# Weight conversion popped two pieces a step from step 29 to step 65, and one batch's second mixing half at two tasks a step

## The chip, the cores and the metric

The kernel runs on one core of one Trainium2 chip. The metric is the device time of one launch in microseconds (us), the median of several runs of the same program; lower is better.

## The reference

Three layers follow each other, all in float32. The first is causal attention over 4 batches, 8 heads, 576 positions and head width 64, with a bias from a running sum:

```python
cum = np.cumsum(np.maximum(s, 0.0), axis=-1)
bias = -(cum[:, :, :, None] - cum[:, :, None, :])
scores = np.where(causal, -1e9, scale * q @ k.T + np.minimum(bias, 0.0))   # softmax, then @ v
```

The second takes the attention output as x (4 x 576 x 512) and has two parts, a low-rank mixing over positions and a feed-forward net (FFN) of width 2048:

```python
u = x + ((x.T @ U) @ V).T          # mixing, rank 32
x = u + np.maximum(u @ w_ch1, 0.0) @ w_ch2
```

The third is a mixture of four attention experts of width 64 with top-2 gates over the same 576 positions. The weights U, V, w_ch1 and w_ch2 arrive as 64-bit floats, so the kernel turns them into 32-bit floats itself, by bit operations, and splits each operand of a matmul into a high and a low part (three matmuls stand for one).

## The kernel before

The program is written in an explicit order: each engine works through its instructions in the order in which the Python code records them, and waits where one needs another engine's result. TensorE (PE) does the matmuls and transposes, VectorE (DVE) and ScalarE (ACT) empty its results and do the softmax, GpSimd (POOL) scales the softmax rows and takes the low parts of the FFN weights, and SyncE (SP) issues all DMAs, in one line.

**Steps.** The first phase is a loop (`Attn.run`) over 160 steps, one for each of the 5 row blocks of the 32 heads; two heads make a pair, so a pair is 10 steps and a batch 40. A step records the score matmuls of its block (lines 361 and 362), the mask-and-maximum on DVE (line 372, one per step, so it numbers the steps in a trace), the exponential of the step before (line 379), the transposes (402, 405) and the copies out (85, 87) of the block ten steps back, and one piece of the product with V (line 429). Then it calls `fillers(i)`, which adds other work in three kinds:

- a fixed list by step (`todo`): the loads and the operand copies of the next pair, among them the high parts (line 763, POOL), their three copies to other partitions (`place_high`), the low parts (line 667, DVE) and the four last copies (`rest`, which ends with the bias rows, `HI<-Cd`);
- pieces of the weight conversion: a list `convs` of 148 pieces, of which each step takes one, or two in the dense range;
- tasks of mixing and FFN (`background`), as many as the table `BG` says: 1, 1, 0, 2, 1 for the five steps of a head.

```python
for _ in range(CONVS[FAST[0] < i < FAST[1]][i % NT]):
    if i >= 4 and convs:
        convs.pop(0)()
for _ in range(BG[i % NT]):
    background()
```

**Conversion.** 24 jobs: one for U, three for V, four for each of the FFN weights w0 to w4 (256 columns, 256 KB of 64-bit words each). A job is a load (line 186), two operations on ACT (116, 119), three on DVE (122, 126, 130) and, for w0 to w2, the split into a high part on ACT (197) and a low part on POOL (200); w3 and w4 are split later. The pieces of successive jobs are interleaved so that a job takes six pieces. Four buffers hold loaded words.

**Mixing and FFN.** When the second pair of a batch is done, ten mixing tasks of its first half join the queue `mixq`: three of transposes (236) with a copy and a subtraction (240), one product (248) with two empty tasks around it, and four products with an addition into `uT` (259, 262). When the fourth pair is done, the ten of the second half join, the last four of which also split FFN input (276, 277), and then two entries, the second of which puts 14 FFN tasks on `ffnq`. These are, for each of two chunks of 288 positions: a first product for each of w0, w1, w2 (f0 to f2: 12 matmuls at line 293, a relu on ACT at 297 and its low part on DVE at 298) and a second product for each quarter of the output (d0 to d3: 9 matmuls at 307 and an addition at 822; d0 and d1 also split the next chunk's input). An FFN task is taken only when all four jobs of its weight are converted. `background` takes a mixing task on every second call where an FFN task is ready, and the last four mixing tasks of a second half only when `ffnq` is empty.

After step 171 come the remaining 13 weight slices of the FFN over all positions (lines 1010 and 1028), and the third layer.

Of the kernel before, what the change touches and what calls it, by code (L numbers as in the profile page):

```python
# [23 lines left out]
NT = 5  # L24
# [26 lines left out]

PLAIN = (((0, 0),), ((0, 1),), ((0, 2), (1, -2)), ((1, -1),), ((2, -3),), ((0, 3),), ((0, 4),))
STREAM = (((0, 0), (3, -3)), ((-1, 4),), ((0, 1),), ((0, 2), (1, -2)), ((1, -1),), ((0, 3),))
FAST = (40, 70)
RAWS = 4

ENGA = ('vaaaaa', 'aavaav')
ULA = ("vvvv", "gvgg")
# [13 lines left out]
BG = (1, 1, 0, 2, 1)  # L72
# [22 lines left out]
def f32_stages(nc, pool, width, load, m, n, name, use=None, dest=None, fixed={}, raws=2, wide=1):  # L95

    t_ = {}

    def tile_(tag, dt, bufs=1):
        if tag in fixed:
            fixed[tag].append(fixed[tag].pop(0))
            t_[tag] = fixed[tag][-1][:m, :n].bitcast(dt)
            return t_[tag]
        t_[tag] = pool.tile([P, width], dt, tag=tag, name=f"{tag}_{name}", bufs=bufs)[:m, :n]
        return t_[tag]

    def s0():
        raw = pool.tile([P, width], I64, tag="c_raw", name=f"c_raw_{name}", bufs=raws)[:m, :n]  # L110
        load(raw)
        words = raw.bitcast(U32).rearrange("p (n w) -> p n w", w=2)
        t_["low"], t_["high"] = words[:, :, 0], words[:, :, 1].bitcast(F32)

    def p0():
        nc.scalar.activation(out=tile_("c_g", F32, wide), in_=t_["high"], func=AF.Copy, scale=2.0 ** -112)

    def p1():
        nc.scalar.activation(out=tile_("c_r", U32, wide), in_=t_["low"], func=AF.Copy, scale=2.0 ** -29)

    def v0():
        nc.vector.scalar_tensor_tensor(out=tile_("c_s", U32), in0=t_["c_g"].bitcast(U32), scalar=0x80000000,
                                       in1=t_["c_r"], op0=OP.bitwise_and, op1=OP.bitwise_or)

    def v1():
        nc.vector.tensor_scalar(out=tile_("c_a", U32, 2), in0=t_["c_g"].bitcast(U32), scalar1=3, scalar2=None,
                                op0=OP.logical_shift_left)

    def v2():
        nc.vector.tensor_tensor(out=t_["c_a"] if use else dest().bitcast(U32), in0=t_["c_a"], in1=t_["c_s"],  # L130
                                op=OP.add)

    def v3():
        if use:
            t_["u"] = use(t_["c_a"].bitcast(F32))
            next(t_["u"])

    def v4():
        if use:
            next(t_["u"], None)  # L140

    return [s0, p0, p1, (v0, v1, v2, v3, v4)]


def f32_stream(jobs, order):

    n = len(jobs)
    for i in range(-3, n + 1):
        for pieces in order:
            l = [jobs[i + d][3][x] if x >= 0 else jobs[i + d][x + 3] for d, x in pieces if 0 <= i + d < n]  # L150
            if l:
                def step(l=l):
                    for f in l:
                        f()
                yield step
# [3 lines left out]
def fused_kernel(ctx, tc, qk, v, s, u, vv, w12, wp, out):  # L159
# [19 lines left out]
    def wjobs(f, width, cpool, wpool, room, fixed={}, raws=2, wide=1):  # L179


        def job(c0):
            x, c = divmod(c0, DM)

            def load(raw):
                nc.sync.dma_start(out=raw, in_=w12[f, :, x, c:c + width])

            if f in Wf:
                return f32_stages(nc, cpool, room, load, P, width, f"w{f}_{c0}",
                                  dest=lambda: Wf[f][:, x, c:c + width], fixed=fixed, raws=raws, wide=wide)  # L190

            def use(t):
                if c0 == 0:
                    Wh[f] = wpool().tile([P, 2, DM], F32R, tag="wh", name=f"wh_{f}")
                    Wl[f] = wpool().tile([P, 2, DM], F32R, tag="wl", name=f"wl_{f}")
                wh, wl = Wh[f][:, x, c:c + width], Wl[f][:, x, c:c + width]
                nc.scalar.activation(out=wh, in_=t, func=AF.Copy)  # L197
                yield
                eng = nc.vector if WLE == "v" else nc.gpsimd
                eng.tensor_tensor(out=wl, in0=t, in1=wh.bitcast(F32), op=OP.subtract)  # L200
                full[f] = full.get(f, 0) + width

            return f32_stages(nc, cpool, room, load, P, width, f"w{f}_{c0}", use, fixed=fixed, raws=raws, wide=wide)

        return [job(c0) for c0 in range(0, 2 * DM, width)]
# [120 lines left out]
    class Attn:  # L326
# [122 lines left out]
        def run(self, pair_ready, pv_done, heads, fillers):  # L449
            self.pair_ready, self.pv_done, self.heads = pair_ready, pv_done, heads  # L450
            n = len(self.heads) * NT
            i = 0
            while i < n + self.LAG or self.pvq:
                j = i - self.LAG
                view = self.qk(i // NT, i % NT) if i < n else None
                ps = self.tr(j // NT, j % NT) if 0 <= j < n else None
                if i < n:
                    self.peak(i // NT, i % NT, view)
                if 1 <= i <= n:
                    self.exp((i - 1) // NT, (i - 1) % NT)  # L460
                if ps is not None:
                    self.evac(j // NT, j % NT, ps)
                if i % NT == 1 and 1 < i <= n + 1:
                    self.norm(i // NT - 1)
                if self.pvq:
                    self.pvq.pop(0)()
                split = j // (2 * NT) < self.split
                if 0 <= j < n and j % (2 * NT) == 2 * NT - 3 and split:
                    self.push_pv(j // NT, 0)
                if 0 <= j < n and j % (2 * NT) == 2 * NT - 1:  # L470
                    self.push_pv(j // NT, 1 if split else None)
                fillers(i)
                i += 1
# [210 lines left out]
    with ExitStack() as cx:  # L684
# [14 lines left out]
        def load_v(p):  # L699
            b, pr = divmod(p, NP)  # L700
            Vs[p] = d2.tile([P, NT, P], F32, tag="V", name=f"V_{p}")
            nc.sync.dma_start(out=Vs[p], in_=v[b, pr])
# [142 lines left out]
        def use_v(t, x):  # L845
            cs = slice(THIRD * x, THIRD * x + THIRD)
            nc.scalar.activation(out=V4[:, 0, cs], in_=t, func=AF.Copy)
            yield
            nc.vector.tensor_tensor(out=V4[:, 1, cs], in0=t, in1=V4[:, 0, cs].bitcast(F32), op=OP.subtract)

        def job(load, n, name, use):
            return f32_stages(nc, cv, PIECE, load, P, n, name, use, fixed=fixed, raws=RAWS, wide=2)

        jobs = [job(lambda raw: nc.sync.dma_start(out=raw, in_=u), NT * R, "u", use_u)]
        for x in range(S // THIRD):
            jobs.append(job(lambda raw, x=x: nc.sync.dma_start(out=raw, in_=vv[x]), THIRD, f"v{x}",
                            lambda t, x=x: use_v(t, x)))
        jobs += [j for f in range(FA + GROUPS[0]) for j in wjobs(f, PIECE, cv, lambda: w01p, PIECE, fixed, RAWS, 2)]
        convs = list(f32_stream(jobs, STREAM))
# [7 lines left out]
        def background():  # L867


            turn[0] += 1  # L870
            ffn = ffnq and full.get(ffnq[0][0]) == 2 * DM
            if mixq and (turn[0] % 2 or not ffn) and not (mixq[0][1] and ffnq):
                mixq.pop(0)[0]()
            elif ffn:
                ffnq.pop(0)[1]()
# [37 lines left out]
        def fillers(i):  # L913
            p, r = divmod(i, 10)
            now[0] = i % (2 * NT)
            if r == 6 and p < NPR:
                load_v(p)
            if i < 4:
                for _ in range(2):
                    if preps:  # L920
                        preps.pop(0)()
            for x in todo.pop(i, ()):
                x()
            for _ in range(CONVS[FAST[0] < i < FAST[1]][i % NT]):
                if i >= 4 and convs:
                    convs.pop(0)()
            for _ in range(BG[i % NT]):
                background()

        attn.run(pair_ready, pv_done, heads, fillers)  # L930
# [466 lines left out]
```

## Time and profile before

| | us |
|---|---|
| runs (three) | 840.68, 842.06, 843.66 |
| median | 842.06 |
| profiled execution | 842.4 |
| its span, first to last instruction | 840.6 |
| PE busy, share of the span | 799.4, 95% |
| DVE busy | 526.0, 63% |
| ACT busy | 473.8, 56% |
| POOL busy | 322.0, 38% |
| granted TensorE clock | 1.0 |

The score matmuls of the 160 steps start between 9.5 and 269.6 us of the span. Busy shares are averages over stages that differ: in the first phase DVE and ACT are busy for far more than their average. PE busy is the time covered by matmuls that are pipelined and whose ends are modelled; PEld is the loading of their weights, which runs beside them.

### The profile page before, as it was taken

The numbers are of one execution on the slowest core, as the hardware profiler recorded it, in microseconds if no ns is written. First come the engines' busy times: TensorE is split into PE (matmuls) and PEld (weight loads), VectorE is DVE, ScalarE is ACT, GpSimd is POOL, SyncE is SP. The second block draws the span as 40 slices with busy tenths as digits, with TensorE's granted clock in tenths as the row PEclk, the third lists the DMA queues.
The fourth block names the chain that finished last, engine by engine and source line by source line (L and its number), as shares of the span: only waits on it lengthen the run. The fifth ranks groups of instructions, "written<-read, shape, count | busy, mean of one in ns | idle before, by whom it ended". The sixth has DMA issues, their size and how long they took to land.

```text
span 840.6 us, 17207 instructions
## 1 busy us (share of the span) xinstructions
PE 799.4 (95%) x6028; PEld 740.3 (88%) x6028; DVE 526.0 (63%) x1559; ACT 473.8 (56%) x1406; POOL 322.0 (38%) x483
## 2 busy tenths in 40 slices
PE   3889999999999899999999999999999989999997
PEld 2767779889888799999999999999999989898875
DVE  7779987776775357646554764455456775756541
ACT  5779996666776444434444442443334566655662
POOL 5647664453452334223322432232343043322231
PEclk9999999999999999999999999999999999999999
DMA  7887785745741342112111221210000111111221
GB/s 212 216 228 191 212 219 159 202 127 144 190 117 44 106 146 61 51 27 51 51 51 34 69 64 38 52 39 26 1 1 9 36 33 40 48 52 39 76 66 62
DMA packets 37048, 75.44 MB, mean 90 GB/s; under 512 B 4712, under 2 KB 8296, under 8 KB 36932
## 3 DMA queue, kind: packets, MB, share of 16 engines
q1 hardware_dynamic: 36964, 74.36, 32.5%
q8 instruction: 48, 0.79, 0.4%
q14 instruction: 36, 0.29, 0.1%
HBM read 38.93 MB, written 8.55 MB: 56 GB/s over the span
## 4 chain that ended last, share of the span: by engine, by line
PE 79%; DVE 10%; ACT 5%; DMA 3%; issue 2%; SPq 0%; POOL 0%; ACTq 0%; POOLq 0%; DVEq 0%
PE hps L1010 21%; PE facc L1028 21%; PE pv L429 4%; PE qkp L1237 4%; PE facc L307 3%; PE pv L589 3%; PE ops L1264 3%; PE hps L293 3%; PE t L402 3%; PE t L560 2%; PE vps L1171 2%; PE qk L361 2%; PE qk L362 2%; PE t L405 1%; DVE P L372 1%
## 5 line engine op out<-in xcount | busy, mean ns | idle before, releaser
L277 POOL TENSOR_TENSOR ul<-uT,uh 128x288 fp32r<-128x288 f32 x117 | 94.5, 828 | 163.9 <-ACT uh L276 138.1
L1015 DVE SCALAR_TENSOR_TENSOR hl<-hps,hh 128x288 fp32r<-128x288 f32 x110 | 50.3, 457 | 150.1 <-ACT hh L1014 150.1
L390 POOL TENSOR_SCALAR P<-P,stat 64x64 f32<-64x64 f32 (+4 forms) x160 | 101.7, 651 | 104.3 <-DVE stat L385 44.6
L1014 ACT ACTIVATE hh<-hps 128x288 fp32r<-128x288 f32 x110 | 45.0, 409 | 147.9 <-PE hps L1010 147.7
L85 ACT ACTIVATE pt<-t 64x64 f32<-64x64 f32 (+5 forms) x272 | 89.5, 358 | 42.0 <-PE t L405 29.6
L1010 PE MATMUL hps<-uh,wl 128*128 128x288 f32 x376 | 111.2, 296 | 0.0
L1010 PE MATMUL hps<-ul,wh 128*128 128x288 f32 x376 | 111.1, 296 | 0.0
L1028 PE MATMUL facc<-hh,wh 128*128 128x288 f32 x376 | 111.1, 296 | 0.0
L1010 PE MATMUL hps<-uh,wh 128*128 128x288 f32 x376 | 111.0, 295 | 0.0
L1028 PE MATMUL facc<-hh,wl 128*128 128x288 f32 x376 | 110.9, 295 | 0.0
L1028 PE MATMUL facc<-hl,wh 128*128 128x288 f32 x376 | 110.8, 295 | 0.0
L379 ACT ACTIVATE P<-P,stat 64x64 f32<-64x64 f32 (+4 forms) x160 | 89.2, 558 | 23.2 <-DVE stat L372 21.2
L548 POOL TENSOR_SCALAR P<-P,stat,pt 128x128 f32<-128x128 f32 (+4 forms) x72 | 45.8, 653 | 118.1 <-DVE stat L543 54.1
L372 DVE CUSTOM_DVE_ANT_0 P<-qk,mask 64x64 f32<-64x64 f32 (+4 forms) x160 | 77.4, 484 | 13.7 <-PE t L405 8.7
L361 PE MATMUL qk<-R,L 128*128 128x64 f32 (+2 forms) x192 | 66.3, 349 | 18.3 <-DVE L L750 9.6
L200 POOL TENSOR_TENSOR wl<-c_a_w,wh 128x256 fp32r<-128x256 f32 x56 | 43.8, 784 | 73.2 <-ACT wh L197 70.6
L1010 PEld LDWEIGHTS hps<-uh,wl 128*128 128x128 f32 x376 | 70.9, 189 | 0.0
L1028 PEld LDWEIGHTS facc<-hh,wl 128*128 128x128 f32 x376 | 70.9, 188 | 0.0
L1010 PEld LDWEIGHTS hps<-ul,wh 128*128 128x128 f32 x376 | 70.8, 188 | 0.0
L1028 PEld LDWEIGHTS facc<-hl,wh 128*128 128x128 f32 x376 | 70.8, 188 | 0.0
L1028 PEld LDWEIGHTS facc<-hh,wh 128*128 128x128 f32 x376 | 70.6, 188 | 0.1
L1010 PEld LDWEIGHTS hps<-uh,wh 128*128 128x128 f32 x376 | 70.6, 188 | 0.0
(211 smaller groups left out, 2230.0 us busy)
## 6 DMA issues: line engine op xcount, KB each, us to landing
c_raw_w<-in_w_dram SPq DMA_DIRECT2D x64, 256.0 KB
uT<-in_qk_dram SPq DMA_DIRECT2D x15, 576.0 KB
L<-HI SPq DMA_DIRECT2D x28, 288.0 KB
V<-in_v_dram SPq DMA_DIRECT2D x16, 320.0 KB
R<-HI SPq DMA_DIRECT2D x14, 288.0 KB
R<-uT SPq DMA_DIRECT2D x14, 288.0 KB
L<-uT SPq DMA_DIRECT2D x14, 288.0 KB
aD<-stage SPq DMA_DIRECT2D x6, 576.0 KB
```

The source lines that it names most:

```text
L85: nc.scalar.activation(out=out, in_=in_, func=AF.Copy)
L200: eng.tensor_tensor(out=wl, in0=t, in1=wh.bitcast(F32), op=OP.subtract)
L277: eng.tensor_tensor(out=l_, in0=src, in1=h_.bitcast(F32), op=OP.subtract)
L361: nc.tensor.matmul(ps[:, bk, :w], lhsT=q1[:, rows], rhs=k1[:, c0:c0 + w], start=True, stop=False)
L372: nc.vector.tensor_tensor_reduce(out=po, in0=view, in1=mk, scale=-self.scale, scalar=3.0e38, op0=OP.add, op1=OP.min, accum_out=stat[P - M: ...
L379: nc.scalar.activation(out=po, in_=po, func=AF.Exp, scale=-1.0, bias=stat[P - M:, 0, t:t + 1], accum_out=stat[P - M:, 1, t:t + 1])
L390: nc.gpsimd.tensor_scalar(out=pv, in0=pv, scalar1=stat[r0:, 2, t:t + 1], scalar2=1.0 if gate is None else gate(t)[r0:], op0=OP.mult, op1=O ...
L548: nc.gpsimd.tensor_scalar(out=po, in0=po, scalar1=stat[:, 2, s:s + 1], scalar2=1.0 if gate is None else gate(t), op0=OP.mult, op1=OP.mult)
L1010: nc.tensor.matmul(ps, lhsT=w[:, 0, cs], rhs=x, start=i == 0, stop=i == 11)
L1014: nc.scalar.activation(out=hh, in_=ps, func=AF.Relu)
L1015: nc.vector.scalar_tensor_tensor(out=hl, in0=ps, scalar=0.0, in1=hh.bitcast(F32), op0=OP.max, op1=OP.subtract)
L1028: nc.tensor.matmul(accs[c][d], lhsT=w[:, 1, cs], rhs=x, start=f == fs[0] and i == 0, stop=f == fs[-1] and i == 2)
```

## The change

The dense range of the conversion, whose ends are exclusive, is now steps 29 to 65 (before, 41 to 69). A new pair `RUSH` makes `fillers` call `background` twice in each of the steps 52 to 57, whatever `BG` says; step 52 is the one in which the first batch's fourth pair is finished. The lines behind it move down by one.

```diff
-FAST = (40, 70)
+FAST = (28, 66)
 RAWS = 4
+RUSH = (52, 58)
...
-            for _ in range(BG[i % NT]):
+            for _ in range(2 if RUSH[0] <= i < RUSH[1] else BG[i % NT]):
                 background()
```

All 148 pieces of conversion and all tasks stay; only their places change. The conversion's list is used up at step 111 (before, 119).

On DVE, steps 65 and 66 before, where `hl` is the low part after an FFN first product and `c_r_w`, `c_a_w` are of a conversion job:

```order
L372 ISA P_116,stat_110<-qk_0_1438,mask 64x64
L372 ISA stat_110 64x1
L122 SCALAR_TENSOR_TENSOR pt_105<-pt_106,c_r_w_512_1418 128x256
L298 SCALAR_TENSOR_TENSOR hl_1_1467<-hps_1_1453,hh_1_1466 128x288
L372 ISA P_116,stat_110<-qk_1_1470,mask 128x192
L372 ISA stat_110 128x1
L384 TENSOR_SCALAR stat_108<-stat_108 128x5
L385 RECIPROCAL stat_108<-stat_108 128x5
L126 TENSOR_SCALAR c_a_w_512_1490<-pt_106 128x256
L130 ISA c_a_w_512_1490<-c_a_w_512_1490,pt_105 128x512
```

Steps 65 and 66 on DVE now, where `stage` is the result of an FFN second product and `ul` the low part of the next chunk's input:

```order
L373 ISA P_116,stat_110<-qk_0_1477,mask 64x64
L373 ISA stat_110 64x1
L123 SCALAR_TENSOR_TENSOR pt_105<-pt_106,c_r_w_0_1474 128x256
L299 SCALAR_TENSOR_TENSOR hl_2_1506<-hps_2_1492,hh_2_1505 128x288
L373 ISA P_116,stat_110<-qk_1_1509,mask 128x192
L373 ISA stat_110 128x1
L385 TENSOR_SCALAR stat_108<-stat_108 128x5
L386 RECIPROCAL stat_108<-stat_108 128x5
L127 TENSOR_SCALAR c_a_w_0_1529<-pt_106 128x256
L823 TENSOR_TENSOR stage_1541<-facc_0_1531,uT 128x288
L278 TENSOR_TENSOR ul_1_1548<-uT,uh_1_1547 128x288
```

The third first product (`hl_2`) is at step 65, where the second was, and the first second product follows at once; before, the third came at step 73.

On SP's line of DMAs, the copies of pair 4's operands (`HI` high parts, `uT` low parts, `Cd` bias rows), before:

```order
L186 DMA c_raw_w_768_618<-in_w_dram 128x256
L626 DMA L_0_122<-HI 64x1152
L626 DMA L_0_119<-HI 64x1152
L626 DMA R_0_121<-HI 64x1152
L626 DMA R_0_121<-uT 64x2x576
L626 DMA L_0_119<-uT 64x2x576
L626 DMA L_0_122<-Cd 2x2x576
L626 DMA HI<-Cd 4x2x576
L697 DMA uT<-in_qk_dram 128x2x576
```

The same stretch now, from the same load on:

```order
L187 DMA c_raw_w_768_618<-in_w_dram 128x256
L627 DMA L_0_122<-HI 64x1152
L627 DMA L_0_119<-HI 64x1152
L627 DMA R_0_121<-HI 64x1152
L187 DMA c_raw_w_0_690<-in_w_dram 128x256
L627 DMA R_0_121<-uT 64x2x576
L627 DMA L_0_119<-uT 64x2x576
L627 DMA L_0_122<-Cd 2x2x576
L627 DMA HI<-Cd 4x2x576
L698 DMA uT<-in_qk_dram 128x2x576
```

A load of weights now stands between the copies of the high parts and those of the low parts.

## Rows read from the trace of the kernel before

**Rows 1.** The page, part 1: busy us (share of the span) xinstructions.

```profile
PE 799.4 (95%) x6028; PEld 740.3 (88%) x6028; DVE 526.0 (63%) x1559; ACT 473.8 (56%) x1406; POOL 322.0 (38%) x483
```

**Rows 2.** The windows view: a stretch in us, its length, busy us of each engine.

```profile
core 0: us, PE busy (x) PEld busy (x) DVE busy (x) ACT busy (x) POOL busy (x), PEclk, DMA share, GB/s
49.80:65.80 16.00, 15.13 (x118) 11.81 (x118) 13.30 (x43) 12.49 (x42) 10.05 (x15) 1.00 0.66 176
65.80:79.00 13.20, 11.30 (x90) 8.92 (x90) 12.84 (x42) 11.95 (x43) 9.50 (x14) 1.00 0.88 240
79.00:106.70 27.70, 25.89 (x195) 20.68 (x190) 25.36 (x78) 25.46 (x84) 18.07 (x25) 1.00 0.74 193
106.70:131.30 24.60, 24.11 (x189) 19.65 (x189) 20.35 (x67) 20.28 (x69) 16.15 (x24) 1.00 0.72 191
131.30:171.70 40.40, 39.44 (x325) 35.67 (x321) 32.25 (x106) 30.21 (x98) 18.89 (x29) 1.00 0.71 191
171.70:218.60 46.90, 46.54 (x376) 42.88 (x378) 32.16 (x109) 31.34 (x101) 20.91 (x34) 1.00 0.53 148
181.70:201.50 19.80, 19.54 (x162) 17.99 (x161) 13.38 (x45) 13.33 (x42) 8.22 (x13) 1.00 0.54 152
218.60:239.10 20.50, 19.52 (x159) 15.63 (x160) 16.21 (x54) 16.02 (x53) 9.78 (x15) 1.00 0.65 170
234.40:252.20 17.80, 17.46 (x142) 16.29 (x139) 12.61 (x43) 13.00 (x42) 9.63 (x14) 1.00 0.43 104
320.00:340.00 20.00, 20.00 (x152) 20.00 (x151) 14.75 (x32) 8.47 (x24) 8.38 (x11) 1.00 0.24 64
```

**Rows 3.** The windows view of line 372 alone.

```profile
131.30:171.70 40.40, 11.33 (x47) 1.00 0.71 191
```

**Rows 4.** The waits view, 79.0 to 106.7: us in total, times, longest.

```profile
ACT P L379 <- DVE stat L372: 1.6, 4, 0.8
```

**Rows 5.** The waits view, 131.3 to 218.6.

```profile
ACT pt L85 <- PE t L405: 14.8, 7, 3.8
DVE stage L822 <- PE facc L307: 9.7, 9, 2.3
```

**Rows 6.** The lines view, 50 to 79, conversion: xcount | busy us, mean ns.

```profile
L116 ACT ACTIVATE pt<-c_raw_w 128x256 f32<-128x256 f32 x5 | 2.2, 432 | 0.0
L119 ACT ACTIVATE c_r_w<-c_raw_w 128x256 uint32<-128x256 uint32 x5 | 2.2, 441 | 0.0
L197 ACT ACTIVATE wh<-c_a_w 128x256 fp32r<-128x256 f32 x4 | 1.6, 409 | 0.0
L122 DVE SCALAR_TENSOR_TENSOR pt<-pt,c_r_w 128x256 uint32<-128x256 uint32 x4 | 1.7, 431 | 0.0
L126 DVE TENSOR_SCALAR c_a_w<-pt 128x256 uint32<-128x256 uint32 x5 | 2.5, 491 | 0.0
L130 DVE CUSTOM_DVE_ANT_0 c_a_w<-c_a_w,pt 128x512 uint16<-128x512 uint16 x5 | 3.0, 602 | 0.1
```

**Rows 7.** The lines view, 131.3 to 218.6, FFN.

```profile
L297 ACT ACTIVATE hh<-hps 128x288 fp32r<-128x288 f32 x9 | 3.7, 408 | 2.9 <-PE hps L293 2.8
L298 DVE SCALAR_TENSOR_TENSOR hl<-hps,hh 128x288 fp32r<-128x288 f32 x9 | 4.1, 457 | 7.7 <-ACT hh L297 7.6
L822 DVE TENSOR_TENSOR stage<-facc,uT 128x288 f32<-128x288 f32 x13 | 5.9, 455 | 9.8 <-PE facc L307 9.7
```

**Rows 8.** The timeline of SP and PE near steps 30 and 40.

```profile
44.04 0.78 SPq L626 DMA_DIRECT2D HI<-Cd  x1
...
49.12 0.27 PE L362 MATMUL qk<-HI,L 68*128 68x64 f32 x1 [0.40 <-DMA HI<-Cd]
...
57.91 0.52 SPq L626 DMA_DIRECT2D HI<-Cd  x1
...
64.80 1.19 PE L429 MATMUL pv<-pt,V 128*64 128x288 f32 x8
```

## The prediction

> **What bounds the kernel now.** The page's busy shares come first, because they mislead here: PE is at 95% of the span [rows 1], which looks like a kernel with nothing but PE in it. The windows view by stretch comes second [rows 2]. Its stretches are whole numbers of steps: line 372 runs once a step and its accumulator read once more, so 47 instructions in 131.3 to 171.7 are 23 steps and one that reaches in [rows 3]. The stretches are steps 30-39, 40-49, 50-65, 66-80, 81-103 and 104-129, and then, as models, 110-119, 130-142 and 140-149. The last row is the later FFN, where PE never stops: 152 matmuls of 288 columns in 20 us, 0.1316 us each. So a first product of 12 matmuls costs PE 1.58 us and a second product of 9 costs 1.18.
>
> From these rows the reader should see two regimes. In steps 40-65 DVE and ACT are the bound: 12.84 and 11.95 of 13.2 us, then 25.36 and 25.46 of 27.7 [rows 2], and the waits view agrees, since ACT's largest wait there is 1.6 us, for DVE [rows 4]. In steps 81-129 DVE falls to 80% and 69% while PE's weight loads rise from 75% to 88% and 91% [rows 2], and now DVE and ACT wait for PE: 14.8 us for transposes and 9.7 for second products [rows 5]. Steps 66-80 are the change from one to the other. After step 129 neither kernel has a task waiting until pair 11 is done at step 132, and the order from there on is the same but for two tasks that change places and one that is done earlier. So what the change is worth is the time at which step 130 starts, 218.6 us now; the rest of the span is shifted by it.
>
> **The change part by part.** Popping the two queues step by step through both programs gives the contents of each stretch.
>
> *Steps 30-49 and the pops beside them.* Steps 29-40 take one more piece each, 12 pieces, which is two jobs. A job costs ACT 0.432 + 0.441 + 0.409 = 1.28 us and DVE 0.431 + 0.491 + 0.602 = 1.52 [rows 6]; two jobs cost DVE 3.0. Steps 30-39 get ten of the twelve pieces: DVE goes from 13.30 to 15.8 us of work in 16.0 us. At the 97% that steps 40-49 reach with DVE (12.84 of 13.2) that needs 16.3 us; but part of DVE's idle time there lies behind late operands and stays. I take +0.8, and +0.4 for the two pieces outside. Bounds: 0 (all of it falls into the 2.7 us that DVE idles) and +3.0 (none does). **+1.2.**
>
> *The loads.* A load of 256 KB now stands between pair 4's high copies and its low copies on SP, and the next ones come three to six steps earlier. The copies behind it end with the bias rows, issued at 57.91. At step 30 the same copy was issued at 44.04, and PE waited for it until 49.12, 5.1 us [rows 8]. So pair 4's lands at about 63.0, while PE is busy with products until about 66 and step 40 begins then [rows 8]: some 2.8 us to spare. One load in the line would have to delay it by more than that, and DMA's share in steps 30-39 is 0.66, the lowest of the early rows. I price it at 0, with 1.5 us as the other end.
>
> *Steps 50-65.* The ten mixing tasks of the second half, the two empty entries and f0, f1 were spread over steps 53-65; now all twelve queue entries are in steps 52-57, f0 and f1 at 58, and steps 59-64 have no task, because f2 needs w2, whose last piece is popped at step 65. So the contents of the stretch stay, with f2 added: DVE 0.457, ACT 0.408 [rows 7]. DVE and ACT are at 92% either way, and crowding the work into one half and thinning the other moves no sum; in steps 59-64 PE has idle time that it had in 66-72 before. **+0.5**, from -1 (the last idle 8% shrinks) to +2 (two mixing tasks in a step stall each other).
>
> *Steps 66-80.* Before: f2, d0-d2, three transposes, one product 248. Now: d0-d3, f0-f2, d0-d3 and three transposes. That adds 2 first and 5 second products, 2 x 1.58 + 5 x 1.18 = 9.1 us of PE, and drops the product 248 (10 matmuls, 1.3 at the same rate): +7.8 on PE. DVE gets 2 x 0.457 + 5 x 0.455 = 3.2 [rows 7] and loses four pieces, 1.0: from 20.35 to 22.6 of 24.6. So the stretch becomes one of PE. Models are steps 140-149 (3 first, 3 second products in 17.8 us) and 110-119 (the same and three transposes in 19.8) [rows 2]. One and a half of the first is 26.7 us with 4.5 of each kind; 1.5 first products fewer and 3.5 second more add 1.8: 28.5. From the second, 31.5. Steps 66-80 lie nearer to the first, since both models hold the long product with V done in one piece, and up to pair 6 it comes in two. I take 29.0, **+4.4**; ends +2.2 (only DVE counts) and +6.9.
>
> By PE's own busy time, 24.11 of 24.6, this stretch has no room at all, and the 7.8 us would be added in full. The Trainium skill's page "Perfetto Trace Analysis", section "Identifying the Most-Contended Engine", says that matmul busy time does not show how near PE is to its limit, since matmuls are pipelined, and that the share of LDWEIGHTS does. By that, 19.65 of 24.6, there are 4.95 us of room, and the stretch would grow by 2.9 instead of 4.4; the sum below would then be +0.3, by busy time +5.2. The models from the trace stand between them, nearer to the skill's.
>
> *Steps 81-103.* Before: d3 of the first chunk, f0-f2 and d0-d3 of the second (3 first and 5 second products), and mixing. Now mixing alone (the product 248 too): PE loses 3 x 1.58 + 5 x 1.18 - 1.3 = 9.3 us, and steps 88-92 have no task, because pair 7 is not done. With that little, PE is no longer the bound and the 9.3 us don't come back in full. Models: steps 130-142, mixing alone, 1.58 us a step (20.5 / 13); steps 30-39 with one piece a step and mixing, 1.60; the fastest, steps 40-49, 1.32 [rows 2]. At 1.59, 23 steps take 36.5 us instead of 40.4: **-3.9**. Ends: -7.0 (1.45 a step) and -2.4 (1.65).
>
> *Steps 104-129.* The same 14 FFN and 10 mixing tasks, two steps ahead, and eight pieces of conversion fewer on DVE and ACT, which are not the bound: **-0.4**, from -1.5 to +0.5.
>
> Sum: 1.2 + 0.5 + 4.4 - 3.9 - 0.4 = +1.8 us. The profiled execution took 842.4 us, 1.8 above its span and 0.3 above the median of the runs; against the median the sum gives 843.9, and I say 844.0. About 0.3%, 2.5 us, is what a measurement of this kernel can tell from no change, so the likeliest case is none that can be told, on the slow side. Its own range is 841 to 846.5.
>
> **The rivals.**
>
> *Faster: the light steps run fast.* If steps 81-103 keep the pace of 1.45, because without FFN nothing in PE's line delays the transposes that ACT waited 14.8 us for, they give back 7.0. With steps 66-80 at 28.0 (+3.4) and the early pops in DVE's idle time (+0.3) the sum is 0.3 + 0.5 + 3.4 - 7.0 - 0.7 = -3.5: 838.6. For it: steps 40-49 with two pieces a step do 1.32. Against it: they have two mixing tasks where 81-103 have some eighteen, and steps 130-142, with mixing and no pieces at all, do 1.58.
>
> *Slower: FFN is bunched and then runs dry.* The mechanism is the place of the 7 FFN tasks: they meet in steps 66-80, which become purely a matter of PE at the pace of steps 110-119 (+6.5), and are missing in 88-92 and 128-129, where a step can't get shorter than its softmax (-3.0). With +1.5 in steps 30-49 and +0.8 in 50-65 and -0.4 that is +5.4: 847.4. It decides once steps 66-80 take over 30.5 us. For it: PE's matmuls in the two models are at 98% busy; against it: steps 66-80 have spare DVE time and short products with V.
>
> *Late operands.* The load in front of pair 4's low copies delays them past the 2.8 us; then PE waits at step 40, as it did at step 30, and so again at pair 5: +1.5 each at most, on top of +1.8: 847. Nothing in the row of step 40 speaks for it but the delay of 5.1 us at step 30.
>
> *The second knob does nothing.* Done at two tasks a step or not, f2 waits for w2 until step 65, so the mixing's early end is worth one step at most; then the conversion alone decides, +1.2 against some of the -0.4, and the time is 843. This falls into the likeliest case.
>
> **How the numbers follow.** Likeliest, with the idle second knob inside it: 0.45. Faster: 0.24. Slower by bunching: 0.25; late operands: 0.06. From the likeliest case a few parts in 45 pass the bound of 2.5 us, more upward than downward, since its sum is at +1.8: faster by over 0.3% 0.25, within 0.3% 0.41, slower by over 0.3% 0.34. The sums of all low and all high ends are -7 and +11; such a meeting is rare, and 8 in 10 lie between -5.5 and +7.5: 836.5 to 849.5.
>
> **What would show it right or wrong.** In the changed profile step 40 should start near 67 us, step 66 near 108.4, step 81 near 137.4, step 104 near 174 and step 130 near 220.4. PE should show no wait for `HI<-Cd` at step 40. Weight loads of PE should rise in steps 66-80 to about 90% and fall in 81-103 to about 76%, as in steps 130-142. The forecast is wrong if step 130 starts before 216 or after 223, if steps 30-49 grow by over 3 us, or if the part after step 130 changes its length by more than 1 us.

## The result and the profile after

The changed kernel takes 850.67 us (median of 4 runs, 847.65 to 855.62), the kernel before 842.86 on the same chip (840.68 to 844.29): ratio 1.0096, 95% interval 1.0072 to 1.0119. It is slower, and above the range of 836.5 to 849.5 us. The profiled execution took 852.27 us with a span of 850.2; before, 842.4 and 840.6. The two profiles lie 9.6 us apart and the medians 7.8: the traced execution of the kernel before has no fall of the TensorE clock ahead of its last 0.7 us, while other executions of it have mean granted clocks down to 0.992, so a difference between two profiles is not yet the price in the median.

The page of the changed kernel, parts 1 and 2: busy time (share of the span), and the granted TensorE clock in 40 slices.

```profile
PE 805.5 (95%) x6028; PEld 742.2 (87%) x6028; DVE 524.7 (62%) x1559; ACT 474.6 (56%) x1406; POOL 319.9 (38%) x483
...
PEclk9999999999899999999999999999999999999999
```

Every engine has as many instructions as before. The windows view of the changed kernel (same columns as [rows 2]) has the steps 30-39, 40-49, 50-65, 66-80, 81-103, 104-129 and 130-140; the last two rows are steps 66-72 and 4 us behind the start of step 130. Lines are one higher than before.

```profile
50.60:67.50 16.90, 15.35 (x119) 11.72 (x115) 15.86 (x48) 15.14 (x51) 11.66 (x17) 1.00 0.79 197
67.50:80.50 13.00, 10.87 (x86) 8.64 (x88) 12.67 (x41) 11.62 (x42) 9.35 (x14) 1.00 0.83 215
80.50:109.80 29.30, 27.07 (x207) 22.38 (x203) 25.92 (x81) 25.86 (x85) 18.24 (x25) 1.00 0.73 191
109.80:140.70 30.90, 30.81 (x245) 27.33 (x244) 20.69 (x70) 20.54 (x66) 13.64 (x22) 1.00 0.60 165
140.70:176.30 35.60, 33.77 (x256) 26.84 (x255) 29.92 (x101) 28.53 (x93) 18.34 (x29) 1.00 0.71 187
176.30:225.10 48.80, 46.61 (x372) 42.74 (x371) 30.33 (x103) 31.24 (x102) 19.80 (x33) 0.98 0.55 151
225.10:246.00 20.90, 20.25 (x151) 15.39 (x150) 14.12 (x49) 14.05 (x47) 8.18 (x14) 0.88 0.54 144
...
109.80:126.40 16.60, 16.51 (x131) 14.55 (x131) 10.23 (x36) 9.63 (x32) 9.59 (x15) 1.00 0.67 183
...
224.00:228.00 4.00, 3.91 (x23) 2.95 (x25) 1.78 (x9) 1.47 (x6) 1.13 (x2) 0.50 0.44 166
```

| steps | before | after | difference | forecast |
|---|---|---|---|---|
| up to 29 | 49.8 | 50.6 | +0.8 | +0.4 |
| 30-49 | 29.2 | 29.9 | +0.7 | +0.8 |
| 50-65 | 27.7 | 29.3 | +1.6 | +0.5 |
| 66-80 | 24.6 | 30.9 | +6.3 | +4.4 |
| 81-103 | 40.4 | 35.6 | -4.8 | -3.9 |
| 104-129 | 46.9 | 48.8 | +1.9 | -0.4 |
| 130 to the end | 622.0 | 625.1 | +3.1 | 0 |

Two places stand out: steps 66-80, and the surroundings of step 130, where nothing was expected.

**Steps 66-72** hold all of the +6.3 and 1.0 us more, since the eight behind them give that back. The same seven steps in the kernel before:

```profile
106.70:116.00 9.30, 9.07 (x74) 6.78 (x73) 9.07 (x32) 8.93 (x33) 7.09 (x11) 1.00 0.71 201
```

They go from 9.3 to 16.6 us. DVE was busy for 9.07 of 9.3 us, 98% (PE's matmuls for as much, its weight loads for 73%); now DVE is at 62%, PE at 99% and the weight loads at 88%. The waits view of the changed kernel, 109.8 to 140.7 (what waits, for whom: us in total, times, longest), says the same: DVE and ACT now wait for the FFN.

```profile
DVE hl L299 <- ACT hh L298: 5.2, 4, 2.2
...
ACT hh L298 <- PE hps L294: 4.9, 2, 2.9
DVE stage L823 <- PE facc L308: 3.0, 5, 0.8
```

What was added there is in the lines view of the same stretch (operation, xcount | busy us, mean ns); these are one of three matmuls of each kind of FFN product:

```profile
L294 PE MATMUL hps<-uh,wh 128*128 128x288 f32 x10 | 3.2, 325 | 0.0
L308 PE MATMUL facc<-hh,wh 128*128 128x288 f32 x10 | 3.2, 324 | 0.4 <-ACT hh L298 0.4
```

That is 60 FFN matmuls, where the kernel before had 4 in these steps. At 0.1316 us each, the 56 more are 7.4 us, and the steps are 7.3 longer.

**Step 130.** Timelines (start, length, engine, line, operation). On SP in the changed kernel, pair 13's operands; step 130 is the first that reads them:

```profile
216.68 0.57 SPq L825 DMA_DIRECT2D aD<-stage  x1
217.35 0.61 SPq L627 DMA_DIRECT2D R<-uT  x1
218.02 1.05 SPq L627 DMA_DIRECT2D L<-uT  x1
219.12 1.11 SPq L627 DMA_DIRECT2D L<-Cd  x1
220.34 1.01 SPq L627 DMA_DIRECT2D HI<-Cd  x1
```

On SP in the kernel before:

```profile
208.97 0.62 SPq L626 DMA_DIRECT2D R<-uT  x1
209.63 0.62 SPq L626 DMA_DIRECT2D L<-uT  x1
210.29 0.72 SPq L626 DMA_DIRECT2D L<-Cd  x1
211.11 1.05 SPq L626 DMA_DIRECT2D HI<-Cd  x1
...
216.88 0.57 SPq L824 DMA_DIRECT2D aD<-stage  x1
```

`aD<-stage` stores a finished FFN chunk. It is recorded when the chunk's last second product is emptied: step 128 before, step 123 now, since the FFN is ahead. The copies `R<-uT` to `HI<-Cd` are recorded at step 124. So the store now stands ahead of them, SP waits for it, and the copies wait with it. SP's waits and the low parts on DVE, in the changed kernel:

```profile
SPq L825 <- DVE stage L823: 6.9, 1, 6.9
```

```profile
214.49 0.76 DVE L668 TENSOR_TENSOR uT<-uT,HI 128x576 fp32r<-128x576 f32 x1
```

The low parts are there at 215.25; the first copy leaves at 217.35, 2.1 us later. Step 128 has one mixing task left and step 129 no task at all, so PE has nothing to cover that with. PE in the changed kernel ([..] is idle time and what ended it):

```profile
221.24 0.27 PE L406 MATMUL t<-ident,P 128*64 128x128 f32 x1
223.27 0.42 PE L362 MATMUL qk<-R,L 128*128 128x64 f32 x1 [1.76 <-DMA L<-uT]
224.09 0.39 PE L363 MATMUL qk<-HI,L 68*128 68x64 f32 x1 [0.39 <-issue]
...
226.14 4.84 PE L430 MATMUL pv<-pt,V 128*64 128x288 f32 x32
```

The wait costs 2.1 us. Behind it the granted clock is at 0.50 (1.2 GHz) from 223.1 to 229.95, and the 32 matmuls of a product with V take 4.84 us; before they take 2.99:

```profile
218.52 2.99 PE L429 MATMUL pv<-pt,V 128*64 128x288 f32 x32
```

### The profile page after: what moved, and what is told of

Same layout as the page of the kernel before. It is cut to its first block, busy times and chain, and to the rows that moved or that the text cites. A ratio compares the mean times of both kernels' runs of the same rounds, so it can differ in the third digit from the quotient of the medians.

```text
span 850.2 us, 17207 instructions
## 1 busy us (share of the span) xinstructions
PE 805.5 (95%) x6028; PEld 742.2 (87%) x6028; DVE 524.7 (62%) x1559; ACT 474.6 (56%) x1406; POOL 319.9 (38%) x483
## 4 chain that ended last, share of the span: by engine, by line
PE 80%; DVE 10%; ACT 5%; issue 3%; DMA 2%; SPq 0%; POOL 0%; ACTq 0%; DVEq 0%; POOLq 0%
PE hps L1011 21%; PE facc L1029 20%; PE pv L430 5%; PE qkp L1238 4%; PE hps L294 3%; PE t L403 3%; PE facc L308 3%; PE pv L590 3%; PE ops L1265 3%; PE t L561 2%; PE vps L1172 2%; PE qk L362 2%; PE qk L363 2%; PE t L406 1%; DVE P L373 1%
## 5 line engine op out<-in xcount | busy, mean ns | idle before, releaser
L391 POOL TENSOR_SCALAR P<-P,stat 64x64 f32<-64x64 f32 (+4 forms) x160 | 99.5, 636 | 118.7 <-DVE stat L386 41.5
L373 DVE CUSTOM_DVE_ANT_0 P<-qk,mask 64x64 f32<-64x64 f32 (+4 forms) x160 | 77.3, 484 | 19.9 <-PE t L406 11.8
```

Source lines behind the costliest of these rows:

```text
L373: nc.vector.tensor_tensor_reduce(out=po, in0=view, in1=mk, scale=-self.scale, scalar=3.0e38, op0=OP.add, op1=OP.min, accum_out=stat[P - M: ...
L391: nc.gpsimd.tensor_scalar(out=pv, in0=pv, scalar1=stat[r0:, 2, t:t + 1], scalar2=1.0 if gate is None else gate(t)[r0:], op0=OP.mult, op1=O ...
```

## The experiments

Times are medians, ratios are to the kernel before on the same chip, with 95% intervals. Lengths of steps are from each kernel's profile.

**The two halves of the change.** E1 has the early conversion alone (without `RUSH`), E2 `RUSH` alone (`FAST` as before), E9 the early conversion with the first batch's FFN kept out of steps 66-72.

```diff
 E2: -FAST = (28, 66)                                        +FAST = (40, 70)
 E9: -ffn = ffnq and full.get(ffnq[0][0]) == 2 * DM
     +ffn = ffnq and full.get(ffnq[0][0]) == 2 * DM and not 66 <= stp[0] < 73
```

> The earlier dense range alone, without the doubled mixing. Theory A (bunching): the FFN of the first batch starts at step 66 instead of 73, and nine of its twelve remaining tasks stand in steps 66 to 79, so steps 66 to 80 grow by 3 to 5 us and the light steps 81 to 103 give back about 4. Theory B (the store in front): the store of the second batch's second chunk is still recorded at step 123, ahead of pair 13's low copies at step 124, so PE waits at step 130 for 2 us or more and the clock may fall there, 2.5 to 5.5 us. A and B together: 846 to 850 us. Theory C (conversion is dear where DVE is the bound, and nothing else matters): 844 us, without a wait at step 130.

> The doubled mixing of steps 52 to 57 alone, with the dense range of before. Two FFN tasks come earlier (steps 58 and 59), the third waits for its weight until step 73 as before. Theory A (bunching) and theory B (the store in front, which here is recorded at step 126, behind pair 13's copies) both expect no change: 841 to 844 us, step 130 at 217 to 221 us of the span. If crowding the mixing into steps that DVE and ACT bind costs by itself, steps 50 to 65 grow by 1.5 us as in the changed kernel, and the time is 844 to 845.

> The earlier dense range alone, with every FFN and mixing task in the step where the kernel before has it (the third FFN task is held until step 73). What is left is the price of early conversion. Theory C (twelve pieces more in steps 29 to 40, on DVE and ACT that are the bound there, and no return later, where PE is the bound): steps 30 to 66 grow by 1.5 to 2.5 us, nothing is given back, 844.5 to 846. As I predicted (1.2 us, 0.4 of it given back): 843.5 to 844.5. If conversion has no price: 842 to 843.5.

E1: 853.64 us, 1.0125 (1.0104 to 1.0145): over the 846 to 850 of its two theories together, and no better than the whole change (0.3% above it, with intervals that overlap). E2: 843.99, 1.0003 (0.9992 to 1.0015). E9: 843.98, 1.0009 (0.9998 to 1.0020); its steps 66-72 in the windows view:

```profile
108.20:116.90 8.70, 8.49 (x71) 6.28 (x70) 7.69 (x30) 7.34 (x26) 6.61 (x11) 1.00 0.69 191
```

So `RUSH` alone is worth nothing, and converting early costs some 0.8 us by itself, with an interval that reaches down to no cost. What costs is that finished weights let the FFN tasks come earlier: in E1's trace the third one is emptied at step 66 (before, 73) and the last at step 83 (before, 95). Why E1 is no better than the whole change was open until E13.

**What sets the length of steps 66-72.** E8 leaves out two of the three matmuls of each FFN product of the first batch (the correcting ones). E6 empties each FFN result one step later than it is made, E7 does that in the kernel before.

```diff
 E8: +ws = ((Wh[f], h_), (Wh[f], l_), (Wl[f], h_))[:1 if c < 2 else 3]
 E6, E7: +late.append(empty)        # run at the next step
```

> The changed kernel with a third of the matmuls of the first batch's 14 FFN tasks (the high parts' product alone; the two correcting products are left out), and ACT's, DVE's and POOL's work as it is. In steps 66 to 80 PE does 9.5 us less. If PE's matmuls are what those steps last for: they shrink by 8 to 9.5 us, to 22 us. If the hand-offs between PE, ACT and DVE are: they shrink by under 5 us, and 26 us or more stay.

> The changed kernel, but the operations that empty an FFN task's result (relu and low part, or the addition into stage) are recorded in the next step, behind that step's mask and maximum, not right behind the task's matmuls. Hand-off theory (an FFN task stands in line between two steps on PE, ACT and DVE alike, so that DVE and ACT idle through its matmuls): steps 66 to 80 shrink from 31 to 26 to 28 us, and the total to 843 to 847. If steps 66 to 80 are simply full of PE work: no gain beyond 1 us, 849 to 851.

> The kernel before with the emptying of FFN results one step later, as in the run above. Hand-off theory: the steps with FFN tasks (73 to 95, 106 to 128, 144 to 161) get shorter by 0.1 to 0.3 us each, 835 to 841 us. If PE's own work is the bound there: 842 to 845.

E8's steps 66-72:

```profile
107.90:119.70 11.80, 11.80 (x98) 9.86 (x96) 10.47 (x36) 9.72 (x34) 9.72 (x15) 1.00 0.71 198
```

They take 11.8 us instead of 16.6, 4.8 less, for 5.3 us of PE work taken out (40 of the 60 matmuls at 0.1316); steps 66-80 take 23.5 instead of 30.9. So PE's matmuls set these steps, in the main: the 7.4 us that steps 66-80 give back are a little less than the 8 to 9.5 of that forecast, and more than the 5 of the other. Its time, 846.94 us, 1.0045 (1.0023 to 1.0067), gives back only 4.3 us by the ratios, of the 12.6 taken out of the whole batch (two thirds of 6 x 1.58 + 8 x 1.18); its ten runs lie between 842.12 (the traced one) and 850.39 us, with mean granted clocks of 0.988 to 0.996, so the total is not a clean price. E6: 850.40, 1.0090 (1.0068 to 1.0112), no gain, and steps 66-72 take 19.1 us. Its total holds a second thing: one step later, the last store stands behind pair 13's copies (on SP at 222.10 us, the first of the low copies at 218.24), so steps 125-134 take 13.7 us instead of 18.9, while emptying late makes steps 66-80 3.1 us longer. E7: 846.12, 1.0033 (1.0022 to 1.0044), slower and above both of its forecasts; why is open. The theory that DVE and ACT wait because a result is emptied too soon falls.

**The store in SP's line.** E5 moves one store, that of the second batch's second chunk, behind pair 13's copies; E3 delays all stores to the sixth step of a pair; E11 leaves the store and adds 18 matmuls, whose result nothing reads, at step 129.

```diff
 E5: +if c == 3:
     +    todo.setdefault(125, []).append(store)
     +else:
     +    store()
 E3: +stores.append((c, stage["t"]))      # handed to SP at r == 5
 E11: +if i == 129:
      +    for _ in range(18):
      +        nc.tensor.matmul(ps, lhsT=V4[:, 0, :P], rhs=V4[:, 0, :CH], start=True, stop=True)
```

> The changed kernel with the store of the fourth chunk alone handed to SP at step 125, behind pair 13's last copies; the three other stores stay where the change has them, so no store is forced to stand right before the next chunk's first result, as in the kernel with all stores late. Store in front: from step 125 to step 135 the time is that of the kernel before (15.5 us) instead of 19.0, PE has no wait for L<-uT at step 130, the clock doesn't fall there, and the total is 2 to 5 us under the changed kernel: 845.5 to 848.5. If the wait at step 130 was hidden anyway: 850.

> The changed kernel with one thing moved: the store of an FFN chunk is handed to SP at the sixth step of a pair, behind the last copies of the next pair's operands, instead of at once. Theory B: pair 13's low copies are issued as soon as they are computed, PE does not wait for them at step 130 and the granted clock stays at 1.0 there; 2.5 to 5.5 us less than the changed kernel, 845 to 848 us. Theory A alone (all of the loss is from bunching): no difference, 849 to 851.

> The changed kernel with 18 matmuls added at step 129, whose result nobody reads (2.4 us of PE in front of the scores of step 130). PE works while it would wait for pair 13's low copies. If the fall of the granted clock behind that wait is what costs 3 us after step 130: the clock stays at 1.0 there, step 131 takes 2.7 us instead of 5.6, and the total is 1.5 to 3 us under the changed kernel, 847.5 to 849, though work was added. If the clock falls for another reason, or costs nothing: 850 to 852.

E5: 847.79 us, 1.0051 (1.0032 to 1.0069). SP and PE in its timeline:

```profile
216.71 0.62 SPq L627 DMA_DIRECT2D R<-uT  x1
...
220.57 1.39 SPq L826 DMA_DIRECT2D aD<-stage  x1
```

```profile
222.70 0.28 PE L362 MATMUL qk<-R,L 128*128 128x64 f32 x1
```

No wait at step 130 and no fall of the clock there; steps 125-134 take 13.8 us instead of 18.9 (before, 15.5). That is 5.1 us in the profiles; the ratios differ by 0.45%, 3.8 us. The steps 66-72 stay at 16.7.

E3: 856.44, 1.0159 (1.0144 to 1.0174), above both of its forecasts. The gain at step 130 is there too (steps 125-134 take 13.8), but `stage` has one buffer, and with the store just ahead of the next chunk's first result, that result waits for it: steps 73-74 take 10.1 us instead of 3.8. The run shows the price of another wait and is no verdict on the store. E11: 850.55, 1.0094 (1.0080 to 1.0109). In its profile PE has no wait for a DMA at step 130 and the clock stays at 1.00:

```profile
221.64 2.61 PE L928 MATMUL fill<-V 128*128 128x288 f32 x18
...
225.54 2.99 PE L430 MATMUL pv<-pt,V 128*64 128x288 f32 x32
```

Steps 125-134 take 16.1 us, so with the gap filled the clock stays, as the first forecast has it, but the ratio is that of the changed kernel, as the second has it: the filling takes 2.6 us itself, and two of the changed kernel's four runs have mean granted clocks of 0.998 and 1.000, so the fall is not in each of them.

The runs with a mean granted clock of 1.000 show the store's price almost without falls: 847.65 us for the change, 845.34 for E5, and 841.97 and 841.77 for the kernel before, measured beside E5. By these single runs the store costs 2.3 us, close to PE's wait of 2.1, and the falls behind that wait would make up the rest of the 3.8.

**The conversion alone, with two stores moved.** In E1's trace the same thing happens twice. At step 90, SP and then PE:

```profile
144.76 0.57 SPq L824 DMA_DIRECT2D aD<-stage  x1
145.38 0.63 SPq L626 DMA_DIRECT2D R<-uT  x1
```

```profile
151.32 0.27 PE L361 MATMUL qk<-R,L 128*128 128x64 f32 x1 [1.40 <-DMA L<-uT]
152.47 0.39 PE L362 MATMUL qk<-HI,L 68*128 68x64 f32 x1 [0.88 <-DMA HI<-Cd]
```

Behind it the clock is at 0.50 from 152.2 to 159.0, and again from 227.3 to 234.1 behind step 130. In the changed kernel the store near step 90 stands ahead of the copies too, but leaves before they are ready:

```profile
140.81 1.14 SPq L825 DMA_DIRECT2D aD<-stage  x1
...
145.58 0.62 SPq L627 DMA_DIRECT2D R<-uT  x1
```

E13 is E1 with both stores behind the copies:

```diff
+if c in (1, 3):
+    todo.setdefault({1: 85, 3: 125}[c], []).append(store)
```

> Only the dense conversion from step 29 to step 65, as in the first experiment, and two of the stores of FFN chunks put behind the operand copies of pairs 9 and 13 on SP's line (steps 85 and 125). In the first experiment's profile PE waits 1.4 + 0.9 us at step 90 for copies that stand behind a store, and at step 130 again, and the granted clock falls to 0.5 for 6.8 us behind each; steps 88 to 93 gain 1.9 us on before, where the changed kernel's give back 3.3, and steps 125 to 135 lose 3.5. If the stores in SP's line are why the conversion alone is slower than the whole change, both waits and both falls go, steps 88 to 93 give back about 3, steps 125 to 135 lose nothing, and the time is 845 to 847.5 (+0.3% to +0.55%). If the conversion costs this by itself, the waits go and the time stays above 850.

E13: 848.09 us, 1.0048 (1.0034 to 1.0061). On SP and PE at step 90:

```profile
145.52 0.62 SPq L626 DMA_DIRECT2D R<-uT  x1
...
149.39 0.61 SPq L825 DMA_DIRECT2D aD<-stage  x1
```

```profile
152.22 0.27 PE L361 MATMUL qk<-R,L 128*128 128x64 f32 x1
```

Both waits and both falls are gone. Against before, steps 88-92 give back 3.2 us where E1's lose 1.9; steps 125-134 give back 1.8 where E1's lose 3.5. The median is 0.6 us above the range that the store theory gave, and its ratio inside it; the other theory wanted more than 850. With the stores out of the way the conversion alone (1.0048) and the whole change (E5, 1.0051) are the same within their intervals: that is the price of the earlier FFN and conversion, and E9's 1.0009 is the conversion's part in it.

**Versions that might gain.** E4 is the change with no FFN task in steps 59-72, E10 is E5 with an FFN task in every second of these steps, E12 converts later than before (`FAST = (44, 74)`, no `RUSH`).

```diff
 E4:  +... and not 59 <= stp[0] < 73
 E10: +... and (mixq or stp[0] % 2 or not 59 <= stp[0] < 73)
```

> The changed kernel, but no FFN task is taken in steps 59 to 72, so that the third one comes at step 73 as before. The conversion is early and the mixing doubled as in the change; FFN is spread as before, and the second batch's last store is behind pair 13's copies. Theory A: steps 66 to 80 return to about 25 us and the time to 842 to 845. Theory C (early conversion costs): 1 to 3 us stay, 844 to 846. If neither bunching nor the store is the cause, it stays at 849 to 851.

> The changed kernel with the fourth chunk's store late, and the first batch's FFN taken at every second step in 59 to 72, so that it ends at step 88 instead of 80: less bunched, and no four steps without a task at 88 to 91. If bunching and the empty steps after it (with a falling clock) cost beside the store: 1 to 3 us under the kernel with the one store late, 845 to 846.5. If those cancel and only early conversion is left: the same, 847 to 848.

> The kernel before with the dense range four steps later (steps 45 to 73); FFN and mixing tasks keep their steps. Theory C turned round (pieces of conversion leave the early steps that DVE and ACT bind, and come where PE is the bound or near it): 0.5 to 1.5 us less than before, 841 to 842.5. If the early steps have room for them: no change, 842 to 843.5.

E4: 846.79 us, 1.0045 (1.0023 to 1.0067), between its forecasts. E10: 845.08, 1.0029 (1.0018 to 1.0040), with steps 66-72 at 11.0 and 81-103 at 37.9 us. E12: 842.50, 0.9998 (0.9989 to 1.0007). None beats the kernel before. Spreading the FFN seems to take back part of the loss: E10's ratio is 0.22% under E5's, with intervals that overlap, and in the profiles its steps 66-103 take 1.9 us less than E5's. Why E4 stays at +0.45%, where E2 and E9 with one half of it each are at +0.0 and +0.1, is open: in its profile 2.7 of the 5.0 us that it loses behind the start of step 30 arise in steps 30-39, where the clock falls to 0.50 at 51.6; E9 has the same instructions there and loses 0.8.

## Why the prediction was wrong

By the forecast's own signs it is wrong: step 130 starts at 225.1 us (it allowed 216 to 223), and the part behind it grew by 3.1 us (it allowed 1). Its terms one by one:

- **Steps 30-49, the loads.** Right. +0.7 against +0.8 in the profile, and E9 puts the whole of the early conversion at +0.8 us of the median (1.2 - 0.4 forecast). There is no wait at step 40, which starts at 67.5 (67 forecast). The 5.1 us of [rows 8] run from the copy's issue to the matmul's start; PE's own wait in that row is 0.40. The +0.8 before step 30 is not the change, whose instructions are those of before up to step 28: between the traced kernels the start of step 30 differs by 3.2 us (48.8 in E10, 52.0 in E13). In this trace the waits at step 20 come to 1.5 us (before, 0.9), and the clock is at 0.50 for 3.4 us from 35.4.
- **Steps 50-65.** +1.6 instead of +0.5, inside its ends. The two tasks a step make steps 52-57 about 2.3 us longer, and steps 58-65 give back part (E2: all).
- **Steps 66-80: the term that was mis-sized.** +6.3 instead of +4.4, near the end of +6.9, and over the 30.5 us from which "FFN is bunched and then runs dry" decides. In steps 66-72 the 7.4 us of PE work that came in cost 7.3, nearly the full price; E8, by taking such work out, gave 4.8 of 5.3 back. The 30.9 us are nearer to the model of steps 110-119 (31.5) than to the one that was leaned on (28.5), and PE's idle time between weight loads in [rows 2] was not free: steps 66-72 were set by DVE at 98%, and where FFN came in they became PE's entirely. The weight loads of steps 66-80 rose to 88% (90% forecast). The Trainium skill's page "Perfetto Trace Analysis", section "Identifying the Most-Contended Engine", says that the share of weight loads, and not matmul busy time, shows how near PE is to its limit. As the forecast worked it out, that gave +2.9 here and PE's busy time +7.8; the measured +6.3 is nearer to the second, so the trace does not bear the rule out in this stretch.
- **Steps 81-103.** -4.8 against -3.9, weight loads at 75% (76% forecast). 9.3 us of PE work left and half came back, as argued.
- **Steps 104-129 and "the rest of the span is shifted by it": the step that failed.** +1.9 and +3.1, together 5.0, where -0.4 and 0 were forecast. The order around step 130 was taken as the same but for tasks that change places; the move of the store from step 128 to step 123, past the copies of step 124 on SP's line, was not seen, though the forecast did weigh SP's line at step 40. The rival "late operands" had this mechanism, at step 40 and with a load; it came at step 130 with a store. E5 and E13 show it: without the store in front, 847.8 and 848.1 us. That the bunching rival's 847.4 is within 0.1% of both is partly luck: it has +6.5 for steps 66-80, near the measured +6.3, but -3.0 for steps 81-103 (-4.8) and +1.5 for steps 30-49 (+0.7).
- **"The second knob does nothing."** Right alone (E2). In the whole change the store near step 90 leaves before the copies are ready, and in E1, which lacks the knob, behind them; that it is the knob which makes this difference is read from the two traces alone.

In sum: of 7.8 us, some 3.8 are the store in front of the copies, with the falls of the clock behind it (E5), and at most some 0.8 the early conversion (E9). The rest, some 3 us, is put down to the bunched FFN by E13 against E9 (1.0048 against 1.0009), but it is not all located: the profile of the change shows +7.3 us in steps 66-72, but over steps 66-103, where most of that comes back, the net is only 1.5 us (1.5 in E5 too, 1.8 in E13). And E4, with neither the bunched FFN nor a store in front, measured +0.45% too. How this rest divides is open.

## What to carry to other kernels

When work is moved forward, follow its last instruction too: a store on an in-order DMA line is a wait for its source, and every copy recorded behind it waits along. Idle time of an engine in a stretch that another engine bounds is spent at full price once the added work makes it the bound, and the stretch that it left gives back only what that stretch's next bound allows. A light step before a hand-over has nothing to cover a late copy with.

## What the runs showed of the hardware

The granted TensorE clock fell to 0.50 (1.2 GHz) for 3.4 or 6.8 us at a time, at places that differ between kernels. PE had worked little just before: in the 3 us before the fall it was busy for 1.42 us (the change, 223.1), 0.99 (E1, 152.2), 1.28 (E1, 227.3), 1.54 (E5, 75.8) and 1.60 (E2, 107.8), with or without a wait for a DMA; in E3, it had no matmul at all in the 3 us before 134.1. A wait of 2.1 us at step 130 so turned into 5.1 us. Not every such gap has a fall behind it: the kernel before waits 3.2 us for the copies of step 10 and shows no fall in the first phase. E8, with less for PE to do, ran at lower mean clocks than before (0.991 against 0.997, means over its runs and those of before beside it) and returned a third of what it saved; that the one is the reason of the other is not shown.
